# GLA, MoE attention and MLP on one core: MLP rows of eight of nine blocks pass through DRAM in pieces of 32 and VectorE transposes them

## Chip, core and metric
The kernel runs on one core of one Trainium2 chip. The metric is the device time of one execution in microseconds (us); the profiled execution is a separate one, and its span is the time from its first to its last instruction.

## The reference, cut to what matters
Three layers follow each other on 4 batches of 768 positions and 384 features, all in float32. The part that the change touches is the last one:

```python
def _moe2_ref(x, g_ln, w_ch1, w_ch2):          # x: 4 x 768 x 384, w_ch1: 384 x 1536, w_ch2: 1536 x 384
    mu = np.mean(x, axis=-1, keepdims=True)
    var = np.mean((x - mu) ** 2, axis=-1, keepdims=True)
    xn = (x - mu) / np.sqrt(var + 1e-06) * g_ln
    ch = np.maximum(xn @ w_ch1, 0.0) @ w_ch2
    return (x + ch).astype(np.float32)
```

Ahead of it stand a gated linear attention (a recurrence over the positions, 8 heads of 48) and a mixture of four causal softmax attentions, of which each position takes the two best by a gate.

## The kernel before
Matrix products are made of fp32r pieces: each operand is split into a high and a low part, and three products (high by high, low by high, high by low) are added in PSUM.

The program is one list of operations. A planner (Plan.run) keeps a clock for each engine, takes again and again the operation that can start first, by rank among those, and so fixes the order on every engine before anything runs; on the chip each engine then goes through its list strictly in order. An operation's rank is its place in the program plus shifts; the numbers in ORDER are seeds of random shifts for groups among the first 2600 operations (reorder, L156). The planner's costs stand in the calls (a DMA on SP counts 400 ns of SP's time and lands 2.3 us after its bytes).

The stages overlap. Linear attention and the projections (front) run beside the softmax attention of earlier batches until about 250 us; then the attention of the last batch runs beside the first MLP blocks; from about 375 us on only the MLP is left. It works on nine blocks of rows, BLOCKS = (2, 2, 2, 3, 3, 3, 3, 3, 3) tiles of 128 rows (blocks 0 to 8 below). Per block:
- mlp_load (L949): SP loads the rows xt, one DMA a tile, 128 rows of 1536 bytes.
- mlp_ln (L957): VectorE makes mean and variance, and L974 the normalized rows xn, positions on partitions.
- mlp_tr (L977): TensorE transposes them in pieces of 128 by 128 against the identity (L987, three a tile) into a PSUM bank; for each piece ScalarE (L992) writes the high part nh = g * xn, VectorE (L994) the low part nl. Features are on partitions then.
- mlp_1 (L999): for each of 12 groups of 128 hidden features (ff) nine matmuls (L1012) over nh and nl; ScalarE takes the relu hh (L1016), VectorE its low part hl (L1017). Each group takes one of PSUM's 8 banks until its hl is made.
- mlp_2 (L1022): for each tile 36 matmuls (L1031), three an ff, into one bank; VectorE adds xt ("ot", L1038), SP stores the tile (L1040).

back (L1050) lists them so that mlp_ln of the next block comes in the middle of mlp_1, and its mlp_tr between mlp_1 and mlp_2. xn, nh and nl have one buffer for each size of block, xt two (small blocks) or three:

```python
            yield from mlp_1(blk, range(6, KF))
            if nxt:
                yield from mlp_tr(blk + 1)
            yield from mlp_2(blk)
```

Of the kernel before, what the change touches and what calls it, by code (L numbers as in the profile page):

```python
# [69 lines left out]
HOP = {"PE": 53.0, "DVE": 35.0, "ACT": 36.0, "POOL": 76.0, "SP": 60.0, "H": 0.0}  # L70
# [9 lines left out]
def t_dve(n):  # L80
    return 67.0 + n / 0.96
# [202 lines left out]
def kernel(ctx: ExitStack, tc: tile.TileContext, akq, vd, wqkv, wo, g_ln, w1, w2, out):  # L284
# [434 lines left out]
    AA, ATT, OT, RR, M = {}, {}, {}, {}, {}  # L719

    def scores(u):
        b, i, p = UN[u]
        QH, QL, KH, KL, V, W = GEN[b]
        nk = 128 * (i + 1)
        qs = slice(128 * i, 128 * i + 128)
        nm, den, rr = small([128, 2], "nm"), small([128, 2], "den"), small([128, 2, 64], "rr")
# [5 lines left out]
        mx2, dn2 = small([128, 2], "mx2"), small([128, 2, 2], "dn2")  # L732
# [12 lines left out]
        for h in range(2):  # L745
            if wide:
                op("DVE", t_dve(pw), lambda h=h: dve.tensor_reduce(mx2()[:, h:h + 1], P[h][0]()[:, :pw], axis=AX.X, op=OP.max, negate=True),
                   r=[P[h][0]], w=[(mx2, h)], name=f"mx{u}")
            op("DVE", t_dve(pw) + 65, lambda h=h: dve.tensor_tensor_reduce(  # L749
                P[h][-1]()[:, :pw], P[h][-1]()[:, :pw], cmask[:, 512 - pw:], -1.0, mx2()[:, h:h + 1] if wide else 3e38, OP.add, OP.min,  # L750
                nm()[:, h:h + 1]), r=[KC] + ([(mx2, h)] if wide else []), w=[P[h][-1], (nm, h)], name=f"nm{u}")
            for x in range(npc):
                op("ACT", t_act(pw) + 200, lambda h=h, x=x: act.activation(  # L753
                    A[h]()[:, pw * x:pw * x + pw], P[h][x]()[:, :pw], AF.Exp, bias=nm()[:, h:h + 1], scale=1.0 if x < npc - 1 else -1.0,
                    accum_out=dn2()[:, h, x:x + 1] if wide else den()[:, h:h + 1]), r=[P[h][x], (nm, h)],
                   w=[(A[h], x), (dn2, (h, x)) if wide else (den, h)], name=f"E{u}")
        AA[u] = A
        if wide:
            op("DVE", 78, lambda: dve.scalar_tensor_tensor(den(), dn2()[:, :, 0], 1e-9, dn2()[:, :, 1], op0=OP.add, op1=OP.add), r=[dn2], w=[den],
               lock=True, name="dn")  # L760
# [3 lines left out]
        if RRT:  # L764
            m = lambda e: e.tensor_tensor(rr(), den()[:, :, None].to_broadcast([128, 2, 64]),
                                          W()[:, i, 2 * p:2 * p + 2, None].to_broadcast([128, 2, 64]), op=OP.mult)
            if RRA:
                op("POOL", 360, lambda: m(pool), r=[den, (W, i)], w=[rr], name="rr", alt=("DVE", t_dve(128), lambda: m(dve), True) if RRA > 1 else None)
            else:
                op("DVE", t_dve(128), lambda: m(dve), r=[den, (W, i)], w=[rr], lock=True, name="rr")  # L770
        else:
            op("POOL", 200, lambda: pool.tensor_tensor(rr(), den(), W()[:, i, 2 * p:2 * p + 2], op=OP.mult), r=[den, (W, i)], w=[rr], name="rr")
        RR[u] = rr
# [32 lines left out]
    def av(u):  # L806
# [11 lines left out]
        def mm():  # L818
            for x in range(i + 1):
                for h in range(2):  # L820
                    e = 2 * p + h
                    c = 128 * (h * (i + 1) + x)
                    for y in range(0, 64, ws):
                        pe.matmul(O()[64 * h + y:64 * h + y + ws], V()[:, x, HD * e + y:HD * e + y + ws], at()[:, c:c + 128],  # L824
                                  start=(x == 0), stop=(x == i), skip_group_check=True)
            for h in range(0 if RRT else 2):
                for y in range(0, 64, ws):
                    pe.matmul(P()[64 * h + y:64 * h + y + ws, :128], rr()[:, h:h + 1].to_broadcast([128, ws]), ident, start=True, stop=True,
                              skip_group_check=True)

        op("PE", 218 * (i + 2 - RRT), mm, r=([at] if RRT else [KI, rr, at]) + [(V, x) for x in range(i + 1)], w=[P], mode="quad" if AVQ else "pair", name=f"V{u}")
# [125 lines left out]
    def mlp_ln(blk):  # L957
# [256 lines left out]
```

## Time and profile before

| | |
|---|---|
| three runs | 637.08, 637.33, 638.21 us (median 637.33) |
| the profiled execution's own time | 636.82 us |
| its span | 635.1 us |
| busy: TensorE, its weight loads, VectorE, ScalarE, GpSimd | 621.0, 595.7, 425.6, 306.9, 112.4 us |
| granted TensorE clock, mean | 0.995 of full speed |
| DMA: read, written | 46.43 MB, 14.16 MB |

Busy times are sums of instruction durations, overlaps counted once for each engine. A matmul's duration is longer than the distance to the next one, since matmuls are pipelined; how long a row of them holds TensorE is read from the distance of their starts. An arrow (<-) names what ended a wait.

### The profile page before, as it was taken

What the parts mean: (1) busy time and instruction counts of PE and PEld (TensorE: products, weight loads), DVE (VectorE), ACT (ScalarE), POOL (GpSimd) and SP (SyncE); (2) the same over time, 40 slices, a digit from 0 to 9 for tenths busy, and PEclk for the clock granted to TensorE, in tenths of its full rate; (3) what the DMA queues carried; (4) which work ended last, traced back from release to release, by engine and by line L of the source; (5) the groups of instructions that cost most, each with busy time, mean ns of one, the idle gap of its engine ahead of it and who ended that gap; (6) DMA issues with size and microseconds to landing.
All of it is one profiled execution on the core that took longest, in us unless ns stands there. A gap on an engine that the chain in (4) does not pass through costs nothing.

```text
span 635.1 us, 17427 instructions
## 1 busy us (share of the span) xinstructions
PE 621.0 (98%) x7180; PEld 595.7 (94%) x7180; DVE 425.6 (67%) x1270; ACT 306.9 (48%) x868; POOL 112.4 (18%) x162
## 2 busy tenths in 40 slices
PE   6899999999999999999999999999999999999997
PEld 5799998999999999888999999999999999999997
DVE  7999999999999998699996547241534415133221
ACT  4667775668867757688654324130312214022120
POOL 1353433435324322312221000000000000000000
PEclk7999999999999999999999999999999999999999
DMA  8544435453462432972331030001001010000000
GB/s 318 211 156 166 166 108 180 136 174 125 146 222 73 158 97 93 256 199 89 100 101 65 26 124 27 25 2 44 33 25 51 13 62 1 26 13 12 26 1 37
DMA packets 30720, 61.70 MB, mean 97 GB/s; under 512 B 2993, under 2 KB 19889, under 8 KB 30641
## 3 DMA queue, kind: packets, MB, share of 16 engines
q1 hardware_dynamic: 19152, 46.43, 21.9%
q10 hardware_dynamic: 8352, 9.44, 4.2%
q0 software_dynamic: 3136, 4.72, 2.9%
q8 instruction: 56, 0.92, 0.6%
q14 instruction: 24, 0.19, 0.1%
HBM read 46.43 MB, written 14.16 MB: 95 GB/s over the span
## 4 chain that ended last, share of the span: by engine, by line
PE 86%; DVE 7%; DMA 2%; issue 2%; ACT 2%; POOL 1%; SPq 0%; ACTq 0%; DVEq 0%; POOLq 0%
PE F L1031 24%; PE F L1012 22%; PE F L624 7%; PE F L795 5%; PE F L561 5%; PE F L824 5%; PE F L738 4%; PE F L487 4%; PE F L852 4%; PE F L647 3%; PE F L526 2%; PE F L987 1%; PE F L504 1%; DVE F L749 1%; DMA ld<-in_akq_dram 1%
## 5 line engine op out<-in xcount | busy, mean ns | idle before, releaser
L1016 ACT ACTIVATE hh<-F 128x384 fp32r<-128x384 f32 (+1 forms) x108 | 49.0, 455 | 186.4 <-PE F L1012 186.1
L1012 PE MATMUL F<-nh,w1hl 128*128 128x384 f32 (+1 forms) x648 | 118.4, 318 | 0.0
L1017 DVE SCALAR_TENSOR_TENSOR hl<-F,hh 128x384 fp32r<-128x384 f32 (+1 forms) x108 | 55.0, 510 | 73.5 <-ACT hh L1016 73.4
L1012 PEld LDWEIGHTS F<-nh,w1hl 128*128 128x128 f32 x648 | 103.8, 188 | 0.5 <-ACT at L801 0.2
L1031 PE MATMUL F<-w2h,hh 128*128 128x384 f32 x288 | 97.9, 340 | 0.0
L1031 PE MATMUL F<-w2h,hl 128*128 128x384 f32 x288 | 96.8, 336 | 0.0
L1031 PE MATMUL F<-w2l,hh 128*128 128x384 f32 x288 | 96.8, 336 | 0.0
L1038 DVE TENSOR_TENSOR xt<-F,xt 128x384 f32<-128x384 f32 x24 | 13.3, 557 | 99.7 <-PE F L1031 99.7
L753 ACT ACTIVATE A<-F,nm 128x384 f32<-128x384 f32 (+4 forms) x128 | 68.1, 541 | 17.9 <-DVE nm L749 15.8
L1012 PE MATMUL F<-nl,w1hl 128*128 128x384 f32 (+1 forms) x324 | 67.6, 317 | 0.0
L1031 PEld LDWEIGHTS F<-w2h,hh 128*128 128x128 f32 x288 | 54.1, 188 | 0.4 <-issue 0.4
L1031 PEld LDWEIGHTS F<-w2l,hh 128*128 128x128 f32 x288 | 54.2, 188 | 0.0
L1031 PEld LDWEIGHTS F<-w2h,hl 128*128 128x128 f32 x288 | 54.1, 188 | 0.0
L1012 PEld LDWEIGHTS F<-nl,w1hl 128*128 128x128 f32 x324 | 53.7, 188 | 0.0
L795 PE MATMUL F<-ident,A 128*128 128x128 f32 x336 | 50.3, 274 | 0.4 <-DVE smk L494 0.3
L801 ACT ACTIVATE at<-F 128x384 f32<-128x384 f32 (+2 forms) x85 | 41.3, 513 | 12.5 <-PE F L795 10.4
L824 PE MATMUL F<-at,V 128*32 128x128 f32 x1344 | 44.6, 274 | 1.4 <-issue 0.7
L795 PEld LDWEIGHTS F<-ident,A 128*128 128x128 f32 x336 | 38.9, 141 | 3.0 <-issue 0.6
L824 PEld LDWEIGHTS F<-at,V 128*32 128x32 f32 x1344 | 35.6, 110 | 6.5 <-issue 2.6
L468 POOL TENSOR_TENSOR ld<-ld,gt 128x512 f32<-128x512 f32 x22 | 26.2, 1192 | 67.7 <-DVE gt L454 15.1
L561 PE MATMUL F<-smk,vb 128*32 128x128 f32 x768 | 34.8, 279 | 0.4 <-DVE smk L494 0.4
L494 DVE TENSOR_TENSOR smk<-F,gmask 128x512 f32<-128x512 f32 x48 | 31.7, 681 | 0.9 <-PE F L487 0.7
(130 smaller groups left out, 1268.9 us busy)
## 6 DMA issues: line engine op xcount, KB each, us to landing
ld<-in_akq_dram SPq DMA_DIRECT2D x23, 800.0 KB, 5.2
vb<-in_vd_dram SPq DMA_DIRECT2D x24, 256.0 KB, 4.6
raw<-in_w_dram SPq DMA_DIRECT2D x18, 256.0 KB, 2.8
xs<-xo ACTq DMA_DIRECT2D x24, 192.0 KB, 2.6
wsc<-whl ACTq DMA_DIRECT2D x18, 256.0 KB, 2.7
raw<-in_w_dram SPq DMA_DIRECT2D x12, 384.0 KB, 3.5
w1hl<-wsc POOLq DMA_DIRECT2D x4, 1152.0 KB, 10.3
xt<-xs SPq DMA_DIRECT2D x24, 192.0 KB, 3.0
```

Source lines behind the costliest of these rows:

```text
L468: op(qn, t_dve(m) if c < GD else 1150 if m == 512 else 896, lambda js=js, q=q, qe=qe: qe.tensor_tensor(q(), q(), gt()[:, js, 1:], op=OP.mu ...
L494: op("DVE", t_dve(512), lambda h=h: dve.tensor_tensor(sk()[:, h], P[h]().rearrange("p (j t) -> p j t", j=4), gmask[:, None, :].to_broadcas ...
L561: pe.matmul(o, l[x][0], l[x][1], start=(x == 0), stop=(x == len(l) - 1), skip_group_check=True)
L624: pe.matmul(P2()[:, mt % 2], wt()[:, k, cs], x()[:, k, xs_], start=(y == 0 and k == 0), stop=(y == 2 and k == 2))
L753: op("ACT", t_act(pw) + 200, lambda h=h, x=x: act.activation(A[h]()[:, pw * x:pw * x + pw], P[h][x]()[:, :pw], AF.Exp, bias=nm()[:, h:h + ...
L795: pe.transpose(P()[:, 128 * n:128 * n + 128], a, ident)
L801: fa = lambda cs=cs, P=P, n=n: act.activation(at()[:, cs], P()[:, :n], AF.Copy)
L824: pe.matmul(O()[64 * h + y:64 * h + y + ws], V()[:, x, HD * e + y:HD * e + y + ws], at()[:, c:c + 128], start=(x == 0), stop=(x == i), ski ...
L1012: pe.matmul(P()[:, :n], t()[:, w, k, c], x()[:, k], start=(m == 0), stop=(m == 8))
L1016: op("ACT", t_act(n) + 63, lambda P=P, hh=hh: act.activation(hh(), P()[:, :n], AF.Relu), r=[P], w=[hh], name="hh")
L1017: op("DVE", t_dve(n), lambda P=P, hh=hh, hl=hl: dve.scalar_tensor_tensor(hl(), P()[:, :n], 0.0, f(hh()), op0=OP.max, op1=OP.subtract), r=[ ...
L1031: pe.matmul(P()[:, :DM], x()[:, o], W2[w]()[:, ff], start=(ff == 0 and n == 0), stop=(ff == KF - 1 and n == 2))
```

## The change
In blocks 1 to 8 mlp_tr has no TensorE operation any more. mlp_ln stores each tile's xn to a DRAM tensor (L999 of the new file) and loads it back into a new tile sx (L1007) with 12 DMAs a block, one for each of 3 x 4 groups of 32 features. Each DMA fills 32 partitions; its runs are 32 floats (128 bytes) long, 128 rows of a tile times 32 features falling into 4 x 32 runs, so 256 runs a DMA in blocks of two tiles and 384 in blocks of three. What arrives lies so that VectorE's transposition of 32 x 32 squares (L1018, one instruction for each 128 features and the whole block) gives the transposed rows; it writes them into the buffer of xn, after the stores have read it. nh and nl are then made from there, one instruction for each 128 features and block, where there was one for each 128 features and tile. Block 0 keeps TensorE's transposes (L1033). All new DMAs go through SP's queue.

ORDER gets 15 more seeds at its end; the old ones stay. Code for passing the softmax denominators through DRAM comes in too, but its switch RRD is 0, so it does not run; RP's tiles are not made.

```diff
+TRB = 1
+RRD = 0
 SLOTS: "whl": 2, + "sx2": 1, "sx3": 1, "rrb": 3,
+    xnd = dram.tile([B * S, DM], F32, name="xns")
 mlp_ln, after L974:
+            if blk >= TRB:
+                r = slice(128 * (T0[blk] + t), 128 * (T0[blk] + t) + 128)
+                o = op("SP", 400, lambda t=t, r=r: sp.dma_start(xnd[r, :], xn()[:, t]), r=[(xn, t)], w=[(xns, (blk, t))], nbytes=196e3,
+                       name=f"xw{blk}")
...
+        if blk >= TRB:
+            sx = M["sx", blk] = mnew(blk, [128, KT, 128 * nt], F32, "sx")
+            rows = xnd[128 * T0[blk]:128 * (T0[blk] + nt), :].rearrange("(g j) (k q i) -> q k j g i", j=32, k=KT, q=4)
+            for k in range(KT):
+                for q in range(4):
+                    op("SP", 400, lambda k=k, q=q: sp.dma_start(sx()[32 * q:32 * q + 32, k].rearrange("j (g i) -> j g i", i=32), rows[q, k]),
+                       r=[(xns, (blk, t)) for t in range(nt)], w=[(sx, (k, q))], nbytes=49e3 * nt / 3 * 4, name=f"xl{blk}")
 mlp_tr:
+        if blk >= TRB:
...
+            for k in range(KT):
+                op("DVE", t_dve(n), lambda k=k: dve.transpose(xk(k), sx()[:, k]), r=[(sx, (k, q)) for q in range(4)],
+                   w=[(xn, ("k", k))], deps=stores, name="tx")
+                op("ACT", t_act(n) + 50, lambda k=k: act.activation(nh()[:, k], xk(k), AF.Copy, scale=gsb()[:, k:k + 1]),
+                   r=[gsb, (xn, ("k", k))], w=[(nh, (k, t)) for t in range(nt)], name="nh")
+                op("DVE", t_dve(n), lambda k=k: dve.scalar_tensor_tensor(nl()[:, k], xk(k), gsb()[:, k:k + 1], f(nh()[:, k]),
+                                                                         op0=OP.mult, op1=OP.subtract),
...
+                yield 0
+            return
```

Three places show how the order moves. Numbers behind a name tell buffers apart; L1058, L1077, L1084 and L1063 of the new file are L1012, L1031, L1038 and L1017 of the old one. The first is TensorE where mlp_1 of a large block ends and mlp_2 of the same block begins, before and now:

```order
L1012 MATMUL F<-nh_8012,w1hl_5117 128x384 x6
L1012 MATMUL F<-nl_8026,w1hl_5117 128x384 x3
L987 MATMUL F<-ident,xn_8057 128x128 x9
L1031 MATMUL F<-w2h,hh_8179 128x384
L1031 MATMUL F<-w2l,hh_8179 128x384
```
```order
L1058 MATMUL F<-nh_8030,w1hl_5119 128x384 x6
L1058 MATMUL F<-nl_8038,w1hl_5119 128x384 x3
L1077 MATMUL F<-w2h,hh_8193 128x384
L1077 MATMUL F<-w2l,hh_8193 128x384
L1077 MATMUL F<-w2h,hl_8195 128x384
```
The nine transposes between them are gone, and nothing has come in their place.

The second is VectorE at the same boundary, in blocks 4 to 7. Before, with nl of the next block made from PSUM:

```order
L1017 SCALAR_TENSOR_TENSOR hl_8018<-F,hh_8006 128x384
L994 SCALAR_TENSOR_TENSOR nl_8026<-F,gsb,nh_8012 128x128 x9
L974 TENSOR_SCALAR xn_8057<-xt_7854,mv_7901,r_7924 128x384 x3
L1038 TENSOR_TENSOR xt_7156<-F,xt_7156 128x384 x3
L1017 SCALAR_TENSOR_TENSOR hl_8181<-F,hh_8179 128x384
```
```order
L1063 SCALAR_TENSOR_TENSOR hl_8032<-F,hh_8025 128x384
L1022 SCALAR_TENSOR_TENSOR nl_8038<-xn_7717,gsb,nh_8030 128x384 x3
L995 TENSOR_SCALAR xn_8052<-xt_7873,mv_7920,r_7943 128x384 x3
L1084 TENSOR_TENSOR xt_7112<-F,xt_7112 128x384 x2
L1018 STREAM_TRANSPOSE xn_8052<-sx_8092 128x384 x3
L1084 TENSOR_TENSOR xt_7112<-F,xt_7112 128x384
L1063 SCALAR_TENSOR_TENSOR hl_8195<-F,hh_8193 128x384
```
The transposes of the block after next stand between the second and the third tile's addition; nl comes one block later. On SP the same stretch now reads:

```order
L999 DMA xns<-xn_8052 128x384 x3
L1086 DMA out_dram<-xt_7112 128x384
L1007 DMA sx_8092<-xns 32x12x32 x12
L1086 DMA out_dram<-xt_7112 128x384 x2
L975 DMA xt_8211<-xs 128x384 x3
```
The 12 loads stand behind the first tile's store, which waits for that tile's addition.

The third is VectorE at block 2, just after the attention's last product (L859), in the new order:

```order
L859 TENSOR_TENSOR rb<-F,at 128x128
L995 TENSOR_SCALAR xn_6995<-xt_6862,mv_6932,r_6957 128x384 x2
L1063 SCALAR_TENSOR_TENSOR hl_7016<-F,hh_7013 128x256
L1063 SCALAR_TENSOR_TENSOR hl_7027<-F,hh_7025 128x256
L1063 SCALAR_TENSOR_TENSOR hl_7051<-F,hh_7046 128x256
L1018 STREAM_TRANSPOSE xn_6995<-sx_7053 128x256 x3
L1022 SCALAR_TENSOR_TENSOR nl_7134<-xn_6995,gsb,nh_7124 128x256 x3
```
Only three instructions lie here between the rows and their transposition. In the part of TensorE's list ahead of the MLP, five groups of 7 to 24 matmuls have changed places.

## Rows read from the trace of the kernel before
**Rows 1.** The page: span, and the chain that ended last, by engine.
```profile
span 635.1 us, 17427 instructions
...
PE 86%; DVE 7%; DMA 2%; issue 2%; ACT 2%; POOL 1%; SPq 0%; ACTq 0%; DVEq 0%; POOLq 0%
```
**Rows 2.** Stretches (us): busy time of PE, PEld, DVE, ACT, POOL (instructions); clock; DMA.
```profile
300.00:320.00 20.00, 19.60 (x210) 17.78 (x212) 19.53 (x65) 14.46 (x44) 3.47 (x4) 1.00 0.32 91
320.00:340.00 20.00, 20.00 (x223) 18.99 (x216) 17.15 (x57) 9.80 (x28) 5.61 (x7) 1.00 0.26 70
...
420.00:460.00 40.00, 40.00 (x240) 39.93 (x238) 15.07 (x40) 9.45 (x26) 0.00 (x0) 1.00 0.09 30
```
**Rows 3.** The chain in order of time: start, us, engine and line, count.
```profile
316.24 1.01 DVE xn L974
...
323.71 1.04 PE F L852 x6
...
375.91 12.72 PE F L1012 x108
...
478.96 18.72 PE F L1012 x108
497.68 0.98 PE F L987 x9
...
517.39 18.72 PE F L1012 x108
```
**Rows 4.** Line 987, TensorE's transposes: ns shortest, median, longest.
```profile
L987 PE MATMUL F<-ident,xn x72: 270/272/328, 300.3 to 575.2; 128*128 128x128 f32 x72
```
**Rows 5.** TensorE's timeline at block 1's six transposes: start, us.
```profile
317.30 0.94 PE L987 MATMUL F<-ident,xn 128*128 128x128 f32 x6 [0.28 <-DVE xn L974]
317.99 0.42 PE L1031 MATMUL F<-w2h,hh 128*128 128x384 f32 x1
```
**Rows 6.** Groups from 375 us on, by shape: busy us, mean ns | idle before.
```profile
L1017 DVE SCALAR_TENSOR_TENSOR hl<-F,hh 128x384 fp32r<-128x384 f32 x72 | 40.1, 557 | 66.1 <-ACT hh L1016 65.9
L1016 ACT ACTIVATE hh<-F 128x384 fp32r<-128x384 f32 x72 | 35.3, 490 | 166.5 <-PE F L1012 166.5
...
L994 DVE SCALAR_TENSOR_TENSOR nl<-F,gsb,nh 128x128 fp32r<-128x128 f32 x54 | 15.7, 345 | 5.7 <-ACT nh L992 5.6
...
L974 DVE TENSOR_SCALAR xn<-xt,mv,r 128x384 f32<-128x384 f32 x18 | 7.6, 473 | 0.0
...
L1017 DVE SCALAR_TENSOR_TENSOR hl<-F,hh 128x256 fp32r<-128x256 f32 x12 | 5.0, 414 | 1.1 <-ACT hh L1016 1.1
L1016 ACT ACTIVATE hh<-F 128x256 fp32r<-128x256 f32 x12 | 4.6, 382 | 10.2 <-PE F L1012 10.2
```
**Rows 7.** Line 859, stores of 128 rows of 1536 bytes: issue in ns, landing in us.
```profile
L859 ACTq DMA_DIRECT2D xs<-xo x24: 326/326/669, 60.6 to 372.6; - x24
...
DMA to landing us min/median/max: 1.8/2.6/6.3
```
**Rows 8.** Line 899, DMAs of 256 runs of 1024 bytes, likewise.
```profile
L899 ACTq DMA_DIRECT2D wsc<-whl x18: 520/521/580, 61.4 to 253.6; - x18
...
DMA to landing us min/median/max: 2.4/2.7/7.1
```
**Rows 9.** Line 1040, stores of tiles by SP, likewise.
```profile
L1040 SPq DMA_DIRECT2D out_dram<-xt x24: 332/336/430, 343.3 to 632.3; - x24
```
**Rows 10.** The page's DMA queues: packets, MB, share of 16 engines (q1 SP's, q10 ScalarE's).
```profile
q1 hardware_dynamic: 19152, 46.43, 21.9%
q10 hardware_dynamic: 8352, 9.44, 4.2%
```

More of the change, by code (lines that the diff above doesn't have):

```diff
@@ L48 @@
 SGA = 2
-RRA = 2
 GD = 2
@@ L60 @@
 AVQ = 1
-RRT = 1
+TRB = 1
+RRD = 0
+RLAG = 3500.0
+RQ = "SP"
+RL = "SP"
 UPQ = 1
@@ L333 @@
     wsc = T(lambda: None)
+    rrs = T(lambda: None)
+    rrd = dram.tile([B * NSC, 128, 32], F32, name="rrs")
+    xns = T(lambda: None)
+    xnd = dram.tile([B * S, DM], F32, name="xns")
     wscd = dram.tile([128, 2, 3 * DFF], FR, name="wsc")
@@ L398, in set_tri @@
                            channel_multiplier=0)
+    RP = [new("c", [128, 32], F32, f"rp{x}") for x in range(3)]
+    if RRD:
+        for t in RP:
+            op("DVE", 100, lambda t=t: dve.memset(t(), 0.0), w=[t], name="setup")
     op("POOL", 1380, lambda: make_identity(nc, ident), w=[KI], name="setup")
@@ L718 @@
     UN = [(b, i, p) for b in range(B) for i in (range(NSC) if b < B - 1 else reversed(range(NSC))) for p in range(2)]
-    AA, ATT, OT, RR, M = {}, {}, {}, {}, {}
+    AA, ATT, OT, RR, DEN, M = {}, {}, {}, {}, {}, {}
     def scores(u):
@@ L725, in scores @@
         qs = slice(128 * i, 128 * i + 128)
-        nm, den, rr = small([128, 2], "nm"), small([128, 2], "den"), small([128, 2, 64], "rr")
+        nm = small([128, 2], "nm")
+        if p == 0 or not RRD:
+            DEN[u // 2] = small([128, 2, 1 + RRD], "den"), small([128, 2, 1 + RRD, 2], "dn2")
+        den, dn2 = DEN[u // 2]
+        pd = p * RRD
         A = [new("aw", [128, WV + 260], F32, "A", "A") for _ in range(2)]
@@ L731, in scores @@
         P = [[psf() for x in range(npc)] for h in range(2)]
-        mx2, dn2 = small([128, 2], "mx2"), small([128, 2, 2], "dn2")
+        mx2 = small([128, 2], "mx2")
         rs = [slice(64 * h, 64 * h + 64) for h in range(2)]
@@ L754, in scores @@
                     A[h]()[:, pw * x:pw * x + pw], P[h][x]()[:, :pw], AF.Exp, bias=nm()[:, h:h + 1], scale=1.0 if x < npc - 1 else -1.0,
[L755 to L756 removed]
+                    accum_out=dn2()[:, h, pd, x:x + 1] if wide else den()[:, h, pd:pd + 1]), r=[P[h][x], (nm, h)],
+                   w=[(A[h], x), (dn2, (h, pd, x)) if wide else (den, (h, pd))], name=f"E{u}")
         AA[u] = A
+        if pd < RRD:
+            return
+        DEN.pop(u // 2)
         if wide:
[L759 removed]
+            op("DVE", 78, lambda: dve.scalar_tensor_tensor(den(), dn2()[..., 0], 1e-9, dn2()[..., 1], op0=OP.add, op1=OP.add), r=[dn2], w=[den],
                lock=True, name="dn")
@@ L763, in scores @@
         op("DVE", 82, lambda: dve.reciprocal(den(), den()), r=[den], w=[den], name="dn")
[L764 to L773, printed above, removed]
+        if not RRD:
+            rr = RR[u] = small([128, 2, 64], "rr")
+            m = lambda e: e.tensor_tensor(rr(), den().to_broadcast([128, 2, 64]), W()[:, i, 2 * p:2 * p + 2, None].to_broadcast([128, 2, 64]),
+                                          op=OP.mult)
+            op("POOL", 360, lambda: m(pool), r=[den, (W, i)], w=[rr], name="rr", alt=("DVE", t_dve(128), lambda: m(dve), True))
+            return
+        rb, rt = new("aw", [128, 4, 2, 32], F32, "rrb", "rrb"), small([128, 32], "rt")
+        rp, n = RP[u // 2 % 3], u // 2
+        op("DVE", 82, lambda: dve.tensor_tensor(rp()[:, :4].rearrange("t (h p) -> t h p", h=2), den(),
+                                                W()[:, i].rearrange("t (p h) -> t h p", p=2), op=OP.mult), r=[den, (W, i)], w=[rp], lock=True,
+           name="rr")
+        op("DVE", t_dve(32), lambda: dve.transpose(rt(), rp()), r=[rp], w=[rt], name="rrt")
+        op(RQ, 400 if RQ == "SP" else 100, lambda: ENG[RQ].dma_start(rrd[n], rt()), r=[rt], w=[(rrs, n)], nbytes=16e3, lag=RLAG, name=f"rw{n}")
+        for h in range(2):
+            src = rrd[n].rearrange("(b r) j -> b (r j)", r=32)[:, 64 * h:64 * h + 64].rearrange("b (o x) -> o b x", o=1).to_broadcast([64, 4, 64])
+            op(RL, 400 if RL == "SP" else 100, lambda h=h, src=src: ENG[RL].dma_start(rb()[64 * h:64 * h + 64].rearrange("m b p j -> m b (p j)"), src), r=[(rrs, n)],
+               w=[(rb, h)], nbytes=65e3, lag=RLAG, name=f"rl{n}")
+        RR[u - 1] = RR[u] = rb
     def transp(u):
@@ L777, in transp @@
         A = AA.pop(u)
-        at = ATT[u] = new("aw", [128, 2 * S + 128 * RRT], F32, "at", "at")
+        at = ATT[u] = new("aw", [128, 2 * S + 128 * (not RRD)], F32, "at", "at")
         blk = [(h, x) for h in range(2) for x in range(i + 1)]
-        if RRT:
+        if not RRD:
             blk.append((2, 0))
-        rr = RR[u]
+        rr = None if RRD else RR[u]
         wide = i > 3
@@ L785, in transp @@
         ng = (len(blk) + 3) // 4
-        cut = [len(blk) * n // ng for n in range(ng + 1)] if RRT else [min(4 * n, len(blk)) for n in range(ng + 1)]
+        cut = [len(blk) * n // ng for n in range(ng + 1)]
         for x0, x1 in zip(cut, cut[1:]):
@@ L825, in mm @@
                                   start=(x == 0), stop=(x == i), skip_group_check=True)
[L826 to L831, printed above, removed]
+        op("PE", 218 * (i + 1), mm, r=[at] + [(V, x) for x in range(i + 1)], w=[P], mode="quad" if AVQ else "pair", name=f"V{u}")
         rb = new("aw", [128, 128], F32, "rb", "rb")
-        if RRT:
+        if RRD:
+            blocks = lambda x: x.rearrange("e (b j) -> e b j", b=4)
+            op("DVE", t_dve(128), lambda: dve.tensor_tensor(blocks(rb()), blocks(O()), rr()[:, :, p], op=OP.mult), r=[P, rr], w=[rb], name=f"o{u}")
+        else:
             rc = slice(256 * (i + 1), 256 * (i + 1) + 128)
             op("DVE", t_dve(128), lambda: dve.tensor_tensor(rb(), O(), at()[:, rc], op=OP.mult), r=[P, at], w=[rb], name=f"o{u}")
-        else:
-            op("ACT", t_act(128), lambda: act.activation(rb(), P()[:, :128], AF.Copy), r=[P], w=[rb], name=f"rb{u}")
-            op("DVE", t_dve(128), lambda: dve.tensor_tensor(rb(), O(), rb(), op=OP.mult), r=[P, rb], w=[rb], name=f"o{u}")
         op("ACT", 202, lambda: act.activation(oh()[:, p], rb(), AF.Copy), r=[rb], w=[(oh, p)], name=f"oh{u}")
@@ L980, in mlp_tr @@
         nh, nl = M["n", blk] = tuple(mnew(blk, [128, KT, 128 * nt], FR, n) for n in ("nh", "nl"))
+        if blk >= TRB:
+            sx, n, stores = M.pop(("sx", blk)), 128 * nt, M.pop(("xw", blk))
+            xk = lambda k: xn().rearrange("p t (k c) -> p (t k c)", k=KT)[:, n * k:n * k + n]
+            for k in range(KT):
[5 more added lines that the diff above has]
+                                                                         op0=OP.mult, op1=OP.subtract),
+                   r=[gsb, (xn, ("k", k))] + [(nh, (k, t)) for t in range(nt)], w=[(nl, (k, t)) for t in range(nt)], lock=True, name="nl")
+                yield 0
+            return
         for t in range(nt):
```

5 lines of the change are left out of this document (3 added, 2 removed).

## The prediction
> **What bounds the kernel now.** I read the chain that ended last first: 86% of the span is TensorE's, 7% VectorE's [rows 1]. The table of stretches tells where each holds. In the MLP alone (420 to 460 us) TensorE and its weight loads are busy for 40.00 and 39.93 of 40.00 us, VectorE for 15.07, ScalarE for 9.45, GpSimd not at all [rows 2]. So there each TensorE instruction taken out shortens the time by its full length, if nothing new makes TensorE wait. The chain in order of time shows the pattern: 18.72 us of mlp_1, 0.98 us of transposes, 18.7 us of mlp_2, without a gap [rows 3]. Where attention and MLP are mixed it is different: from 300 to 320 us VectorE is busy for 19.53 of 20 us and TensorE for 19.60, so both bind; from 320 us on VectorE has room again (17.15) [rows 2]. The clock is at its upper level (1.00 of 2.4 GHz) in all of these [rows 2].
>
> **What goes.** Before, line 987 has 72 transposes [rows 4], three a tile. Blocks 3 to 8 lose nine each: 6 x 0.98 = 5.9 us [rows 3]. Blocks 1 and 2 lose six each. At block 1 the six hold TensorE from 317.30 to 317.99, 0.69 us [rows 5]; twice that is 1.4 us. There TensorE also stood 0.28 us for xn [rows 5], and VectorE's xn was on the chain [rows 3]; that wait goes, since nothing on TensorE reads xn of block 1 any more: 0.3 us. Together 7.6 us.
>
> **What is added on VectorE and ScalarE.** Per large block nine nl of 345 ns [rows 6] become three of 384 columns, which I price as hl of that size, 557 ns, and three transposes. No row shows one. At least it is a pass over 384 columns from SBUF, 473 ns like xn; at most I give it 1.0 us (two passes); I take 0.56. So 3.1 us of VectorE become 3.4, ScalarE's part shrinks. Both have more than half of their time free there [rows 2], so this costs nothing as long as that cover holds. In the mixed stretch the same sum is 0.4 us for block 1, where VectorE has none to spare; it is in the 0.5 us below.
>
> **What is added on the queues.** Three prices are needed. A store of a tile takes 0.33 us to issue on SP [rows 9] and lands 1.8 to 2.6 us after it [rows 7]. A load issues 256 or 384 runs. A DMA of 128 runs takes 326 ns to issue [rows 7], one of 256 takes 521 [rows 8], 195 ns more for 128 more; so 0.52 us in blocks of two tiles, 0.72 us in blocks of three (at least 0.33, if only the count of DMAs mattered). It lands 2.4 to 2.7 us after issue, like the DMA of 256 runs [rows 8]. The third price, a run of 128 bytes on one of the 16 DMA engines, no row shows. The queues bound it: SP's 19152 packets took 21.9% of 16 x 635.1 us, 116 ns each at 2.4 KB; ScalarE's 8352 took 4.2%, 51 ns each at 1.1 KB [rows 10]. The nearest is 51 ns, the upper end; by bytes it would be 51 x 128 / 1130 = 6 ns, the lower end. The two rows go with the bytes (2.3 times the time for 2.1 times the bytes), so I stay in the lower part: under 30 ns. Up to 30 ns (0.72 us / 24 runs an engine) SP's issue sets the pace, and the exact value drops out.
>
> The Trainium skill (DMA: Bandwidth & Descriptors, Measured) gives about 10.5 ns a packet as its smallest; the estimate by that is 288 x 10.5 ns = 3.0 us for a large block's runs, and the sum stays the same.
>
> **Against what deadlines.** Time runs from the start of a block's first xn.
> - Blocks 5 to 8: SP's list has the first tile's store ahead of the loads, and it waits for that tile's addition, 6.2 us into mlp_2 (a third of 18.7). So the loads start at 6.2 + 0.56 + 0.33 = 7.1 and land at 7.1 + 11 x 0.72 + 2.4 to 2.7 = 17.4 to 17.7; with the last transpose 18.3. VectorE stands at the transposes until then; behind it waits the third tile's addition, due at 18.7. Nothing is late. Were the loads later, the hl of the next mlp_1 would queue behind, and TensorE goes on until PSUM's banks are full: seven groups of 18.72 / 12 = 1.56 us more, to 29.6. nh and nl are made a block later, from data long there.
> - Block 4 has no such wait ahead of its loads, which land at 14 to 15. VectorE reaches its transposes at 14.0 (12 triples of matmuls of 0.52 us in mlp_2 and five groups of 1.56); TensorE would feel it seven groups later, at 24.9.
> - Block 3: xn 3 x 0.47, store to 3.2 to 4.0, loads to 13.5 to 14.6, last transpose, nh and nl 0.56 + 0.49 + 0.56: 15.1 to 16.2. TensorE needs nl after 8 groups of mlp_1 of block 2 (12.72 / 12 = 1.06 us each) and 25 triples of mlp_2 (0.52): 21.5. Spare: over 5 us.
> - Block 2 is the tight one: two xn, 0.95; stores to 2.75 to 3.55; loads 11 x 0.52 + 2.4 to 2.7, to 10.9 to 12.0; then 0.41 + 0.38 + 0.41 [rows 6], done at 12.1 to 13.2. TensorE needs it after 3 groups of 1.06, one output projection of 1.04 [rows 3] and 19 triples of 0.52: 14.1. Spare: 0.9 to 2.0.
> - Block 1: the loads land at 11 to 12 as well, but VectorE gets to the transposes after 26 instructions, 7.8 us at the 0.30 us mean of 300 to 320 us [rows 2], and more if many are long. It may stand there for 0 to 4.5 us. Behind it wait the row maxima of two attention units and pieces of the weight conversion; TensorE reads what comes of them some 54 matmuls later, about 9 us. I take 0.5 us as what reaches TensorE, with 0 and 4.5 as ends.
>
> **Sum.** 636.8 - 7.6 + 0.5 = 629.7 us for the profiled execution; the median of the runs stands 0.5 above it, so 630.2. The new seeds move five small groups of matmuls ahead of the MLP and mix blocks 0 to 2 anew; no row prices that, and I give it 0, with 2 us either way for the range.
>
> **Rivals.**
> - *Partial wait (632 to 636 us).* A run costs about 51 ns, the nearest row. Loads take 9.8 instead of 6.2 us in small blocks, 14.7 instead of 8.6 in large ones. Block 2 is then 1.5 to 2.6 us late, block 3 up to 0.8, block 1 up to 4; the steady blocks land at 24.3, still before 29.6. 2 to 6 us of the 7.6 are given back. For it: two small margins. Against it: the queues' rows go with the bytes.
> - *Slower.* A run costs more than about 55 ns, from where the stalls exceed 7.6 us. At 70 ns: block 1 about 7, block 2 5.7, block 3 5.8, block 4 1.7 us, 20 in all: 649 us. The place is VectorE at the transposes with all behind it. Against it: a run nine times shorter would have to cost more than ScalarE's packets do.
> - *Starved.* The runs cost as much as SP's 2.4 KB packets, 114 to 116 ns. A large block's 288 runs an engine then take 33 us, loads land at 43, 13 us past the deadline, in blocks 5 to 8 each (53 us), and blocks 1 to 4 lose 15 to 19 each: some 750 us. The Trainium skill speaks for this against the change: a plain DMA that transposes by strides is 19 times slower than the crossbar's when the innermost stride is large (VectorE: DVE Perf Modes, The three transpose paths); 19 times 6 ns is 114 ns. But here the innermost runs are 32 contiguous floats on both sides. No row here shows either.
> - *More (627 to 629 us).* The new order also closes gaps at 283 to 320 us, where VectorE binds. TensorE is idle for only 0.4 of the 20 us [rows 2], which speaks against much.
> - *The change does less than it says:* if block 0's kind of transposes remained in others. The new order has only six of them; no chance given.
>
> **Numbers.** A measurement of this kernel tells about 0.2%, 1.3 us, from no change. Forecast (629 to 632) 0.62, more 0.10, partial wait 0.17, slower 0.08, starved 0.03. Faster: 0.62 + 0.10 + 0.14 of the partial wait = 0.86; same 0.04; slower 0.10. The range goes from 628.2 (2 us of order) to 634.8 (two thirds of the partial wait); it leaves out the two slow cases (0.11) and about 0.04 each of the partial wait and of the rival with more.
>
> **What would show it.** Right: six matmuls in the transposes' line instead of 72; mlp_1 and mlp_2 of large blocks following each other without a break, 37.4 us a block instead of 38.4; loads at 0.5 and 0.7 us of SP each, landing within 3 us; VectorE standing at the transposes, the third tile's addition not late. Wrong: TensorE waiting for nl at the start of a block's mlp_1, first in block 2; hl late behind transposes with TensorE waiting for a PSUM bank; loads whose landing grows from the first to the twelfth, which would mean runs over 30 ns.

## The result: 630.04 us, 0.988 of the time before

The changed kernel takes 630.04 us (median of 4 runs, 628.73 to 630.76) beside 637.77 us of the kernel before in the same comparison (637.08 to 638.31); the ratio is 0.9877, 95% interval 0.9857 to 0.9897. The profiled executions are 636.82 and 630.18 us, 6.64 us apart.

The page of the changed kernel: span, SP's queue (packets, MB, share of 16 engines), and the chain by engine, against [rows 1, 10].

```profile
span 628.5 us, 17407 instructions
...
q1 hardware_dynamic: 57648, 55.09, 28.3%
...
PE 86%; DVE 6%; DMA 4%; SPq 1%; issue 1%; POOL 1%; ACT 1%; DVEq 0%; POOLq 0%
```

The same stretches as in [rows 2], and one of 3 us in which SP issues loads:

```profile
300.00:320.00 20.00, 19.99 (x225) 19.11 (x225) 18.46 (x60) 12.21 (x37) 5.28 (x7) 1.00 0.37 102
320.00:340.00 20.00, 19.02 (x171) 17.67 (x171) 17.52 (x56) 11.80 (x35) 4.99 (x6) 1.00 0.35 98
420.00:460.00 40.00, 40.00 (x232) 40.00 (x232) 18.24 (x42) 9.31 (x20) 0.00 (x0) 1.00 0.22 60
...
466.00:469.00 3.00, 3.00 (x19) 3.00 (x18) 0.09 (x1) 0.00 (x0) 0.00 (x0) 1.00 0.61 96
```

The chain in order of time, against [rows 3] (L1058 is mlp_1, L1077 mlp_2):

```profile
437.66 18.72 PE F L1058 x108
456.38 18.73 PE F L1077 x108
475.11 18.72 PE F L1058 x108
...
606.19 18.75 PE F L1077 x108
624.94 0.02 issue
```

mlp_1 and mlp_2 follow each other without the 0.98 us between them: a large block takes 37.45 us, before 38.42. The two programs stand level at 280 us. mlp_1 of block 4 begins at 437.66 instead of 440.54: 2.88 us of gain up to there, of which 1.96 are the transposes of blocks 3 and 4. The rest is what blocks 1 and 2 give: 0.69 and 0.81 us of transposes and 0.28 of the wait for xn [rows 5], with 0.08 by which the changed program is ahead at 281 us, less 0.98 of two new waits (below); that makes 0.88 of the 0.92. The four blocks behind it add 3.9; the last matmul ends 6.8 us earlier. TensorE lost something in the mixed stretch: from 320 to 340 us it is busy for 19.02 us, where it was 20.00. Its timeline has two waits there that it did not have before:

```profile
327.66 0.44 PE L1077 MATMUL F<-w2l,hh 128*128 128x384 f32 x1 [0.24 <-DVE w2l L918]
332.36 0.44 PE L1077 MATMUL F<-w2l,hh 128*128 128x384 f32 x1 [0.74 <-DVE w2l L918]
```

w2l is the low part of W2, which VectorE, ScalarE and GpSimd convert piece by piece in this stretch. VectorE's own timeline shows block 1's transposes ahead of those pieces (first four lines), then block 2 and a steady block:

```profile
323.37 1.10 DVE L1018 STREAM_TRANSPOSE xn<-sx 128x256 f32<-128x256 f32 x3 [0.95 <-DMA sx<-xns]
...
326.05 1.08 DVE L1022 SCALAR_TENSOR_TENSOR nl<-xn,gsb,nh 128x256 fp32r<-128x256 f32 x1
327.06 0.55 DVE L918 TENSOR_TENSOR w2l<-cvu,cva 128x384 fp32r<-128x384 f32 x1
...
331.75 0.56 DVE L918 TENSOR_TENSOR w2l<-cvu,cva 128x384 fp32r<-128x384 f32 x1 [1.21 <-POOL cva L917]
...
368.38 1.45 DVE L1018 STREAM_TRANSPOSE xn<-sx 128x256 f32<-128x256 f32 x3 [4.98 <-DMA sx<-xns]
369.75 1.24 DVE L1022 SCALAR_TENSOR_TENSOR nl<-xn,gsb,nh 128x256 fp32r<-128x256 f32 x3
...
509.88 0.58 DVE L1018 STREAM_TRANSPOSE xn<-sx 128x384 f32<-128x384 f32 x1 [2.02 <-DMA sx<-xns]
512.60 0.56 DVE L1084 TENSOR_TENSOR xt<-F,xt 128x384 f32<-128x384 f32 x1 [2.14 <-PE F L1077]
```

The first of the two pieces stands behind the transposes and one nl; the second waits 1.21 us for GpSimd's part of the conversion (cva), which began only at 330.71, behind work of VectorE's. VectorE stands at the transposes six times, 12.0 us in all, and nearly all of it costs nothing. In block 2 it stands for 4.98 us and nl is ready at 371.0; TensorE begins mlp_1 with nh at 372.24 and reads nl from 372.94, both without a wait. In the steady block the third tile's addition (512.60) waits for TensorE, not for the transposes.

The new operations, by shape, from 375 us on (busy us, mean ns | idle before), and the loads' line (issue in ns, landing in us):

```profile
L1022 DVE SCALAR_TENSOR_TENSOR nl<-xn,gsb,nh 128x384 fp32r<-128x384 f32 x18 | 10.2, 616 | 2.1 <-ACT nh L1020 2.1
L1020 ACT ACTIVATE nh<-xn,gsb 128x384 fp32r<-128x384 f32 x18 | 9.9, 608 | 3.4 <-DVE xn L1018 2.4 <-DMA sx<-xns 1.0
L1018 DVE STREAM_TRANSPOSE xn<-sx 128x384 f32<-128x384 f32 x18 | 9.7, 562 | 6.1 <-DMA sx<-xns 6.1
```
```profile
L1007 SPq DMA_DIRECT2D sx<-xns x96: 303/467/1318, 315.5 to 544.2; - x96
...
DMA to landing us min/median/max: 1.7/2.2/3.6
```

The kernel before made nh from PSUM, in pieces of 128 columns (nl's line is in [rows 6]):

```profile
L992 ACT ACTIVATE nh<-F,gsb 128x128 fp32r<-128x128 f32 x54 | 15.8, 373 | 6.0 <-DVE nl L994 6.0
```

### The profile page after: what moved, and what is told of

It reads as the page before. It is cut to its first block, busy times and chain, and to the rows that moved or that the text cites. A ratio compares the mean times of both kernels' runs of the same rounds, so it can differ in the third digit from the quotient of the medians.

```text
span 628.5 us, 17407 instructions
## 1 busy us (share of the span) xinstructions
PE 615.0 (98%) x7114; PEld 590.2 (94%) x7114; DVE 431.0 (69%) x1246; ACT 300.9 (48%) x829; POOL 114.1 (18%) x165
## 3 DMA queue, kind: packets, MB, share of 16 engines
q1 hardware_dynamic: 57648, 55.09, 28.3%
## 4 chain that ended last, share of the span: by engine, by line
PE 86%; DVE 6%; DMA 4%; SPq 1%; issue 1%; POOL 1%; ACT 1%; DVEq 0%; POOLq 0%
PE F L1077 23%; PE F L1058 22%; PE F L635 8%; PE F L821 5%; PE F L572 5%; PE F L850 5%; PE F L753 4%; PE F L658 4%; PE F L873 4%; PE F L498 3%; PE F L537 1%; DMA raw<-in_w_dram 1%; DMA A<-in_wqkv_dram 1%; PE F L515 1%; DVE F L764 1%
## 5 line engine op out<-in xcount | busy, mean ns | idle before, releaser
L1058 PE MATMUL F<-nh,w1hl 128*128 128x384 f32 (+1 forms) x648 | 118.2, 318 | 0.0
L1063 DVE SCALAR_TENSOR_TENSOR hl<-F,hh 128x384 fp32r<-128x384 f32 (+1 forms) x108 | 55.1, 512 | 80.7 <-ACT hh L1062 80.5
L1058 PEld LDWEIGHTS F<-nh,w1hl 128*128 128x128 f32 x648 | 103.9, 188 | 0.4 <-issue 0.2
L1077 PE MATMUL F<-w2l,hh 128*128 128x384 f32 x288 | 97.0, 337 | 1.0 <-DVE w2l L918 1.0
L1077 PE MATMUL F<-w2h,hh 128*128 128x384 f32 x288 | 97.2, 337 | 0.0
L1077 PE MATMUL F<-w2h,hl 128*128 128x384 f32 x288 | 96.8, 336 | 0.0
L768 ACT ACTIVATE A<-F,nm 128x384 f32<-128x384 f32 (+4 forms) x128 | 68.2, 543 | 15.1 <-DVE nm L764 12.9
L1058 PE MATMUL F<-nl,w1hl 128*128 128x384 f32 (+1 forms) x324 | 67.6, 317 | 0.0
L1084 DVE TENSOR_TENSOR xt<-F,xt 128x384 f32<-128x384 f32 x24 | 13.3, 556 | 73.2 <-PE F L1077 73.2
L1077 PEld LDWEIGHTS F<-w2l,hh 128*128 128x128 f32 x288 | 54.1, 188 | 1.6 <-DVE w2l L918 1.6
L1077 PEld LDWEIGHTS F<-w2h,hh 128*128 128x128 f32 x288 | 54.1, 188 | 0.0
L1077 PEld LDWEIGHTS F<-w2h,hl 128*128 128x128 f32 x288 | 54.1, 188 | 0.0
L1058 PEld LDWEIGHTS F<-nl,w1hl 128*128 128x128 f32 x324 | 53.6, 188 | 0.0
```

The source lines that it names most:

```text
L768: op("ACT", t_act(pw) + 200, lambda h=h, x=x: act.activation(A[h]()[:, pw * x:pw * x + pw], P[h][x]()[:, :pw], AF.Exp, bias=nm()[:, h:h + ...
L1058: pe.matmul(P()[:, :n], t()[:, w, k, c], x()[:, k], start=(m == 0), stop=(m == 8))
L1063: op("DVE", t_dve(n), lambda P=P, hh=hh, hl=hl: dve.scalar_tensor_tensor(hl(), P()[:, :n], 0.0, f(hh()), op0=OP.max, op1=OP.subtract), r=[ ...
L1077: pe.matmul(P()[:, :DM], x()[:, o], W2[w]()[:, ff], start=(ff == 0 and n == 0), stop=(ff == KF - 1 and n == 2))
```

## Experiments

The theory: the gain is the length of the transposes that TensorE no longer does, and the path through DRAM is hidden but for about 1 us at block 1. Its rivals: the gain is the new order's; or the path lies close to its limit.

**The new order without the path** (e1)

```diff
-TRB = 1
+TRB = 9
```


> The 15 new seeds without the path: every block is transposed by TensorE again (72 matmuls in that line, none of the loads). Path theory (the gain is the removed TensorE transposes, the order is worth about nothing): 637.8 us like the kernel before, 636.8 to 638.8, and 38.4 us a large block. Order rival (the seeds hold most of the gain): 630 to 633 us, with the gain made before the first large mlp_1, and a period that is still 38.4.

638.72 us, ratio to before 1.0023 (1.0014 to 1.0033): without the path the new kernel, seeds and idle code, is 1.4 us slower than the one before. The order rival falls. TensorE's timeline names 1.43 of the 2.2 us by which the profiled execution is longer (639.0 against 636.82); where the rest arises stays open. At the start of block 2's mlp_1 it waits for nh, since nothing else is left on its list behind block 2's six transposes.

```profile
375.27 0.82 PE L1033 MATMUL F<-ident,xn 128*128 128x128 f32 x6
377.52 1.26 PE L1058 MATMUL F<-nh,w1hl 128*128 128x256 f32 x6 [1.43 <-ACT nh L1038]
```

**The path with the old seeds** (e2)

```diff
-ORDER = (26, 32, ..., 22586, 30046, ..., 37839,)
+ORDER = (26, 32, ..., 22586,)
```


> The path with the 44 old seeds. Path theory: 637.8 - 7.6 + about 1 at block 1 = 630 to 631.5 us. Order rival: 636 to 638 us. A third, weaker one (the new seeds only make room for the path in the mixed stretch): 632 to 634 us, with VectorE standing longer than 5 us at block 1's or block 2's transposes.

630.88 us, 0.9902 (0.9888 to 0.9915), as the path theory had it. With the old seeds the path brings 6.5 of the 7 to 8 us. With the new seeds the ratio is 0.9877 and, measured again below, 0.9889; the intervals overlap, so that the seeds help beside the path is not shown.

**Only the large blocks through DRAM** (e3), **and block 1 alone back on TensorE** (e4)

```diff
-TRB = 1
+TRB = 3
```


> Blocks 1 and 2 go back to TensorE's transposes, new seeds. By the rows: 630.0 + 2 x 0.69 of transposes + 0.3 of the wait for xn - 1.0 (TensorE's waits for the weight conversion behind block 1's transposes, as the trace after shows them) = 630.7 us, 630.0 to 631.7. If the small blocks gained all that was counted for them: 631.7 or more. If the small blocks were a net loss (block 1's wait larger than what the trace shows): under 629.5.

633.41 us, 0.9942 (0.9930 to 0.9955): 2.7 us above the 630.7 expected. Of the three cases only the open one, 631.7 or more, holds the number, and its terms (twice 0.69 and 0.3 us) stop at 631.7.

```diff
-TRB = 1
+TRB = 2
```


> Block 1 alone goes back to TensorE, new seeds. 630.0 + 0.69 + 0.3 - 1.0 = 630.0 us, 629.4 to 630.8: block 1 through DRAM is about even. If block 1's wait costs nothing: 631.0. If it costs the 4 us that were the upper end: 627 us. VectorE then stands at block 2's transposes alone in the mixed stretch.

630.26 us, 0.9891 (0.9876 to 0.9906), as expected: block 1 is even. TensorE has no wait over 0.2 us behind 300 us, and two groups of three transposes (0.48 and 0.33 us) more. So nearly all that e3 lost comes with block 2, 3.1 us between the medians where I had counted 0.69. Its trace has e1's wait of 1.43 us again, and one more at block 3, whose rows SP loaded late (9 loads of xt from 377.09 us on, 367.85 in the changed kernel, landing in 6.4 us at the median instead of 3.9):

```profile
403.76 1.31 PE L1058 MATMUL F<-nh,w1hl 128*128 128x384 f32 x6 [0.98 <-ACT nh L1020]
```

0.69 + 1.43 + 0.98 = 3.1. (The profiled execution of e3 is 1.3 us above the median, so the third term may be smaller in others.) In the new order the path therefore saves more than TensorE's time at block 2: nh and nl are made while TensorE still has mlp_2 of block 1 to do, where TensorE's own transposes come last and the two engines behind them stand bare. The order makes that wait, not TensorE's transposing as such. The kernel before transposes block 2 earlier and then has 4.68 us of mlp_2 left, up to mlp_1 at 375.91 [rows 3], without a gap:

```profile
368.87 0.48 PE F L987 x3
...
371.23 4.68 PE F L1031 x27
```

Against that kernel block 2 saves its transposes and no more. This fits the path being worth 6.5 us with the old seeds (e2) and 8.5 to 9.3 with the new (e1 beside 0.9889 and 0.9877).

**Only blocks 5 to 8** (e11)

```diff
-TRB = 1
+TRB = 5
```


> Only blocks 5 to 8 pass through DRAM, new seeds. Each block's saving without the mixed stretch: against the run with the new seeds and no block through DRAM (1.0023 of the kernel before) 4 x 0.98 = 3.9 us less, 0.996 to 0.997 of before, 634 to 635 us; the period of the four last blocks 37.45 us, of the others 38.4. If part of the saving is given back in each block (loads late, VectorE late): less than 3 us.

635.73 us, 0.9970 (0.9959 to 0.9981), at the end of what was expected, 0.0053 below e1: 3.4 us. In the traces, where the start of the run is out of it, block 4's mlp_1 to the last matmul's end takes 187.29 us here (443.12 to 630.41) and 191.18 in e1 (442.72 to 633.90): 3.89 us for four blocks, 0.97 each. Nothing is given back in the steady stage.

**Shorter runs: 64 and 32 bytes** (e5, e6). The store lays the tile out in 2 or 4 column parts, the loads fetch as many more, shorter runs. The values arrive in another arrangement, so these two kernels compute something else; bytes, DMAs and planned order stay. The cut of e5 (e6 has RH = 4), its lines shortened:

```diff
+RH = 2
-sp.dma_start(xnd[r, :], xn()[:, t])
+sp.dma_start(pieces(blk).rearrange("(h t p) c -> t p h c", h=RH, p=128)[t], xn()[:, t].rearrange("p (h c) -> p h c", h=RH))
...
-rows = xnd[...].rearrange("(g j) (k q i) -> q k j g i", j=32, k=KT, q=4)
+rows = pieces(blk).rearrange("(x j) (k q i) -> q k j x i", j=32, k=KT, q=4)
```


> Twice as many runs, each half as long (64 bytes), same bytes and same number of DMAs; the same planned order. The transposes then see the pieces in another arrangement, so the output is not the reference's. Theory (a run costs well under 20 ns, and the issue of a DMA on SP, 0.49 us at 256 and at 384 runs, sets the pace): loads still issue every 0.5 us and land within 3 us, 629.5 to 631.5 us, 37.45 us a large block. If a run costs 20 ns, the most that the trace after leaves open (24 runs an engine in 0.49 us): a large block's 576 runs take 11.5 us, the twelfth lands 5 us or more after its issue, block 2 about 0.5 us late, 631 to 633 us. If the issue grows with the runs as I extrapolated before (0.195 us for 128): 0.91 and 1.30 us a load, 11 and 15.6 us a block, block 2 and block 3 late by 4 and 5: 636 to 640 us.

631.25 us, 0.9911 (0.9896 to 0.9925). A steady block's 12 loads take 6.83 us of SP instead of 6.07, the landing 2.4 instead of 2.2 us; the period stays 37.45 us and block 2 is not late, as expected. What the trace shows it to cost is at block 1, where TensorE's waits for w2l grow from 0.24 and 0.74 to 0.96 and 0.71 us.

> Four times as many runs of 32 bytes (1024 a load in small blocks, 1536 in large ones; 96 an engine and load), again with the same bytes, DMAs and order, and an output in another arrangement. By the theory the path must break somewhere here: it stays hidden only while a run costs under 0.49 / 96 = 5 ns. At 10 ns a large block's loads take 11.5 us and a small one's 7.7: block 2 0.5 us late, block 3 at its limit, 630.5 to 633 us. At 20 ns 23 and 15.4 us: block 2 8 us late, block 3 12, block 1 some 8, block 4 and the steady blocks 3 each: 660 us or more. VectorE stands at the transposes in each case; TensorE feels it first in block 2 and block 3, last in the steady blocks, whose limit is 29.6 us after the first xn.

636.18 us, 0.9990 (0.9981 to 0.9999): here the gain is used up. The expectation missed it: the loads came out as in its case of 10 ns a run (10.78 and 8.05 us for 11.5 and 7.7), for which it gave 630.5 to 633. The loads' line with 64 and with 32 bytes, and one stretch of loads of each (the last figures are the DMA share and GB/s):

```profile
L1011 SPq DMA_DIRECT2D sx<-xns x96: 303/524/1510, 316.2 to 546.4; - x96
...
DMA to landing us min/median/max: 2.0/2.4/4.3
```
```profile
L1011 SPq DMA_DIRECT2D sx<-xns x96: 320/791/1953, 316.0 to 555.2; - x96
...
DMA to landing us min/median/max: 2.4/3.2/4.3
```
```profile
466.00:469.00 3.00, 3.00 (x20) 3.00 (x19) 0.00 (x0) 0.00 (x0) 0.00 (x0) 1.00 0.85 82
```
```profile
472.00:475.00 3.00, 3.00 (x19) 3.00 (x18) 0.00 (x0) 0.00 (x0) 0.00 (x0) 1.00 0.91 52
```

A large block's load puts 24, 48 or 96 runs on each of 16 engines. The 12 loads take 6.07, 6.83 and 10.78 us, so 0.51, 0.57 and 0.90 us a load; times the DMA share of 0.61, 0.85 and 0.91 and divided by the runs that is, as an estimate, 12.9, 10.1 and 8.5 ns a run. SP's queue as a whole agrees: it moves the same 55.09 MB in 109824 packets more with 32 bytes, at 36.3% instead of 28.3% of 16 engines, which is 7.7 ns for each packet added.

```profile
q1 hardware_dynamic: 167472, 55.09, 36.3%
```

At 128 bytes the engines have room and a load takes what SP's issue takes; at 32 bytes they are nearly full, and the longer issue fits SP waiting for them. TensorE's timeline and the stretches of e6 show where it breaks, in block 1 and in block 2 and in no block behind them:

```profile
328.17 0.44 PE L1081 MATMUL F<-w2h,hh 128*128 128x384 f32 x1 [0.90 <-ACT w2h L917]
330.32 0.45 PE L1081 MATMUL F<-w2l,hh 128*128 128x384 f32 x1 [1.71 <-DVE w2l L919]
...
332.47 0.52 PE L1081 MATMUL F<-w2l,hh 128*128 128x384 f32 x1
332.79 0.52 PE L1081 MATMUL F<-w2h,hl 128*128 128x384 f32 x1
...
377.47 0.98 PE L1062 MATMUL F<-nh,w1hl 128*128 128x256 f32 x6 [1.84 <-ACT nh L1024]
```
```profile
328.00:330.00 2.00, 0.44 (x1) 0.19 (x1) 2.00 (x5) 2.00 (x8) 1.00 (x1) 1.00 0.54 141
332.00:334.00 2.00, 2.00 (x8) 2.00 (x7) 1.20 (x6) 0.74 (x2) 0.62 (x1) 0.50 0.23 22
376.00:378.00 2.00, 0.53 (x4) 0.54 (x5) 1.57 (x5) 0.71 (x2) 0.00 (x0) 1.00 0.93 291
380.00:382.00 2.00, 2.00 (x11) 2.00 (x11) 1.83 (x8) 0.75 (x3) 0.00 (x0) 0.50 0.89 312
```

The span is 6.8 us longer than the changed kernel's. The waits are 1.6 us more at block 1 (0.90 + 1.71 - 0.24 - 0.74) and 1.8 at block 2. The clock takes about as much: behind block 1's two waits and behind block 2's the granted clock falls to 0.50 of 2.4 GHz, so 1.2 GHz, and matmuls of 384 columns start 0.32 us apart instead of 0.17. Block 2's first three groups of mlp_1 take 4.8 us instead of 3.2, and some ten matmuls at 332 us 0.15 us more each: 3.1 us.

**Block 0 through DRAM as well** (e7)

```diff
-TRB = 1
+TRB = 0
```


> Block 0 through DRAM as well, new seeds, the mixed stretch planned anew. TensorE loses six transposes (0.48 + 0.33 = 0.8 us in the chain of the run with block 1 on TensorE). Theory: the path from xn to nl takes about 10 us, and at block 0 only attention is there to cover it, where VectorE binds: at best even, 630 to 633 us. Rival (every transposition taken from TensorE shortens the time): 629.2 us.

634.49 us, 0.9961 (0.9948 to 0.9974): 4 to 5 us above the changed kernel, more than I gave it. Block 0's xn is made at 299.4 us and transposed from 310.8 on, and mlp_1 begins at 315.30; with TensorE's transposes it begins at 303.95. Little covers the path there: from 300 to 320 us TensorE is busy for 18.65 us instead of 19.99, at a mean clock of 0.91 (0.50 from 307 to 310 us).

```profile
300.00:320.00 20.00, 18.65 (x219) 15.81 (x218) 19.84 (x69) 13.77 (x41) 5.58 (x9) 0.91 0.53 133
```

Then the chain runs over SP's queue, with block 1's store and the rows of W2 waiting to be loaded, to the conversion of W2 and to a wait of TensorE of 1.62 us before 340.91:

```profile
316.94 3.97 DMA xns<-xn
...
327.71 3.59 DMA raw<-in_w_dram
...
340.91 1.74 PE F L850 x56
```

**Block 1's microsecond** (e8, e10). First the planner's price for a load, then the planner's landing time for block 1's loads:

```diff
-op("SP", 400, lambda k=k, q=q: sp.dma_start(sx()...
+op("SP", 490, lambda k=k, q=q: sp.dma_start(sx()...
```


> The planner counts 490 ns instead of 400 for a load's issue, which is what SP takes. Its order changes from block 1's second product on. If the 1 us that TensorE lost at block 1 came from transposes that stand too early in VectorE's list: 629.0 to 629.7 us, and VectorE's wait at block 1's transposes under 0.5 us. If it was VectorE's work itself: 630.0, within 0.5. A changed order in a stretch where VectorE binds may cost as much as it gains: 631 at most.

629.90 us, 0.9882 (0.9865 to 0.9898): no difference to the changed kernel that can be told. VectorE still waits 1.04 us at block 1's transposes, and TensorE for w2l once, 1.35 us: the transposes did not move far enough, so this run does not tell the place in VectorE's list from the amount of its work.

```diff
-... nbytes=49e3 * nt / 3 * 4, name=f"xl{blk}")
+... nbytes=49e3 * nt / 3 * 4, lag=(11000.0 if blk == 1 else 2300.0), name=f"xl{blk}")
```


> The planner takes the landing of block 1's loads as 11 instead of 2.3 us, so VectorE's list has block 1's transposes some 20 rows later, behind the two conversions of w2 that TensorE waited for (0.24 and 0.74 us in the trace after). If the 1 us at block 1 is a matter of the place in VectorE's list: 629.0 to 629.6 us, VectorE no longer waits at block 1's transposes, and TensorE's two waits for w2l are gone; TensorE needs block 1's nh and nl only 16 us after the transposes of the trace after, so nothing else is late. If it is the amount of VectorE's work in this stretch, as the run with the load's cost at 490 suggests: 630, within 0.5, and the wait for w2l stands a few pieces later.

> The changed kernel itself, unchanged, beside the run with the later transposes on the same chip: 0.988 of the kernel before, 629 to 630.5 us, by every theory.

630.15 us, 0.9890 (0.9874 to 0.9907), beside 630.28 us, 0.9889 (0.9874 to 0.9904), for the changed kernel on the same chip; 629.0 to 629.6 was expected if the place in the list was the cause. The trace does what was meant: VectorE's transposes come at 330.25 without a wait, and TensorE has no wait left from 320 to 340 us (against 19.02 in the changed kernel).

```profile
330.25 1.09 DVE L1018 STREAM_TRANSPOSE xn<-sx 128x256 f32<-128x256 f32 x3
```
```profile
320.00:340.00 20.00, 20.00 (x183) 19.19 (x183) 18.04 (x59) 12.26 (x35) 5.78 (x7) 1.00 0.38 107
```

Its profiled execution is 628.80 us and block 4's mlp_1 begins 1.33 us earlier than in the repeated changed kernel's, of which 1.05 are that kernel's two waits. But four runs of each spread over 2 us, and the medians agree. So the place in VectorE's list makes the waits in the trace (e4, where VectorE has no transposes in block 1, has none either); that removing them shortens the median is not shown. No version here beats the changed kernel by what can be measured.

## Why the prediction was right, point by point

630.2 us was forecast and 630.04 measured; the steps behind it held unevenly. The mechanism is the one named, but a hit within 0.2 us is partly luck: the sum gave 7.1 us, the profiled executions are 6.64 apart, the medians 7.73, and 7.15 when measured again (e12).

- **What goes.** 0.98 us a large block: right, 0.97 each (the chain, e11). The small blocks' 0.69 each, read at block 1, is right there; block 2's six came in two groups of 0.48 and 0.33 us, so 0.81. Going back to TensorE at block 2 costs more (e3, 3.1 us), but in the new order only. The wait for xn at block 1 [rows 5] is gone.
- **VectorE and ScalarE.** The transpose of 384 columns was taken as 0.56 us and takes 562 ns. nl and nh were priced as hl and hh [rows 6] (557, 490 ns) and take 616 and 608: mis-sized by a tenth and by a quarter. Reading SBUF instead of PSUM need not be the reason. hl and hh, carried on from their 256 and 384 columns to 128, would take 271 and 274 ns (an estimate); nl and nh of the kernel before, from PSUM, took 345 [rows 6] and 373. So most of the surcharge (74 and 99 ns there, 59 and 118 now) was there before; these operations multiply by g, which hl and hh do not. Over a large block, mlp_1 to mlp_1, VectorE's busy time rose from 14.59 to 15.22 us, 0.6 where 0.3 was forecast, and ScalarE's fell from 8.84 to 7.82; the cover held as said. (The 18.24 us from 420 to 460 hold nl of two blocks, at 420.51 and 457.44, and are no measure of it.)
- **The queues.** The term most wrong in size is SP's issue: 0.52 us for 256 runs and 0.72 for 384 were extrapolated from two rows of ScalarE's queue [rows 7, 8]. The 12 loads take 5.83 us in block 2 and 6.07 in a steady block, so about 0.5 us at 256 and at 384 runs; the step with the number of runs was wrong, and harmless, since it erred to the late side. Landing, 2.4 to 2.7 us, was 2.2. A store takes 0.38 instead of 0.33 us.
- **A run's price**, taken below 30 ns between 6 and 51, is about 13 ns. The Trainium skill (DMA: Bandwidth & Descriptors, Measured) has about 10.5 ns a packet, for a DMA of 4 KB from GpSimd's queue: 0.67 us over its 64 packets. That is a price by the packets of a whole DMA, and the prediction used it for the runs of one engine; the 8.5 to 12.9 ns here are for one engine and SP's queue, so that they lie near it confirms nothing.
- **Deadlines.** Block 2: nl 12.2 us after the first xn at 358.8 (forecast 12.1 to 13.2), 1.25 us ahead of mlp_1 (forecast 0.9 to 2.0). Block 3: nl ready at 394.0, used at 399.1, over 5 us as forecast. The steady blocks' last addition is not late; their loads landed well before the forecast, whose clock started 2.8 us too early, at mlp_2 instead of at the first xn (419.45 against 422.22), and whose issue was too long: the last transpose of block 5 ends 12.6 us after the first xn, forecast 18.3.
- **Block 1** was given 0.5 us and cost 0.98, by the mechanism named (the conversion of W2 queued behind the transposes), with VectorE standing 0.95 us of the 0 to 4.5.
- **The new order** was given 0. It costs 1.4 us without the path (e1), with a wait at block 2 that the path takes away; with the path no effect is told from none (e2). For the sum 0 was near enough, though not as "no effect".

Of the rivals, the partial wait came true only in e6, at a quarter of the run length, and mostly where it was worked out: block 2 is 1.8 us late (1.5 to 2.6 forecast) and block 1 makes 2.6 us of waits (up to 4 forecast); the steady blocks, and block 3 too, are never late. There the wait was not the whole price; the clock, which the rival had left out, doubled it. "Starved" supposed 114 ns a run, as the nineteenfold rule for transposing DMAs (the Trainium skill, VectorE: DVE Perf Modes, The three transpose paths) would have it; with contiguous runs of 128 bytes on both sides the measured price is about 13 ns. No run here has the crossbar's transposition to set beside it.

## What to carry to other kernels

Where one engine is busy without a gap, an instruction taken from it is worth its full length, and a detour through DRAM (12.2 us from xn to nl in block 2) is free as long as its deadline lies later: work the deadlines out block by block, and trust the tightest one, not the mean. Issue the detour where the consumer still has a stage of its own to do; where it follows its producer at once (block 0), the detour costs more than it saves. A new order and a new path have to be measured apart and together: here the order alone makes a wait (block 2) that only the path takes away.

## What was not expected of the hardware

- A DMA's issue on SP took about 0.5 us at 256 and at 384 runs; at 768 and 1536 runs, with the 16 engines 0.85 and 0.91 busy, it took 0.57 and 0.90 us.
- Scaled passes over 128x384 (nh, nl) took 608 and 616 ns, where the unscaled ones (hh, hl) took 490 and 557.
- After TensorE had waited 0.90 and 1.71 us with one matmul between, and after 1.84 us (e6), the granted clock fell to 1.2 GHz for some microseconds and the stall's price about doubled. After the wait of 1.43 us in e1 it stayed at 2.4 GHz. The length of one wait does not decide it: in e7 the clock fell after waits of 0.23 and 0.83 us close together (305 to 307 us), and stayed up after one of 1.62 (340.91).
